# Expert scores of two query tiles in three float32r passes over split q and k, in a kernel with a written-out order

## The chip, the core and the metric

The kernel runs on one core of a Trainium2 chip. Its engines are TensorE (PE; its weight loads are listed as PEld), VectorE (DVE), ScalarE (ACT), GpSimd (POOL) and SyncE (SP), which issues the DMAs. The metric is the time of one execution in microseconds on the device, the median of the runs shown.

## The reference, cut to what matters

An attention layer feeds a layer of four experts that are attention layers themselves. With B = 8 batches, 576 tokens and 8 heads of 64:

```python
scores = scale * np.matmul(q, k.transpose(0, 1, 3, 2))     # local mask in heads 0-3, strided in 4-7
x = softmax(scores) @ v                                    # heads side by side: 8 x 576 x 512
logits = x @ w_gate                                        # the two best of E = 4 experts get weights w
for e in range(E):
    q = x @ wq[e]; k = x @ wk[e]; v = x @ wv[e]            # 576 x 64 each
    scores = scale * (q @ k.transpose(0, 2, 1))            # causal
    a = np.exp(scores - max); a /= a.sum(-1, keepdims=True) + 1e-09
    out += w_e * (a @ v @ wo[e])                           # for tokens that chose e
```

All four experts are computed for all tokens; tokens that did not choose an expert get the weight 0. wq and wk are scaled by 8, so the expert scores are far apart and their precision matters.

## The kernel before, in words

**Stage 1** (`stage1`) computes the first attention for a pair of heads: loads, transposes of q and k, block scores, softmax over the blocks, values. Its result stays in SBUF transposed (512 features on partitions, 576 tokens along the row) as two float32r tiles, `xh` (x rounded to float32r) and `xl` (the remainder), which `split` writes (L746, L748). Weights are split likewise. float32r is a 4-byte type of fewer mantissa bits; a product of two split numbers is computed in three passes, h·h, l·h and h·l (`split3`).

**Stage 2** takes the experts in pairs (ep = 0, 1), the two experts of a pair side by side on partitions 0-63 and 64-127. `project` computes q and k of a pair from x: 12 float32r matmuls (4 feature tiles, three passes) into one PSUM bank for each half of 288 tokens (L934; L946 for the very first), and `pj_out` copies the bank to `qk`, a float32 tile of q and k. `values2` computes v and the gate's logits (L876, L846) and the gate's weights.

`attend` computes the expert scores by tiles of 128 queries and all keys up to the diagonal. Tiles 0 and 1 share one operation (`s2q`, L1001). Tile 2 has 384 keys and tile 3 has 512; each is one operation `s2` (L1013): for each expert a of the pair, one float32 matmul of 64 rows, in the tile shape 64x128, in which the array holds two halves. So there are 8 x 2 x 2 = 32 such operations. The last 64 queries of both pairs share two operations `s2_4` (L1035). Masking and the maximum are one VectorE instruction (L970), the exponential runs on ScalarE (L975), the scaling by the gate's weight on GpSimd (L1070). Then come transposes of the probabilities (L1097), the products with v (L1136), another split, and the output projection (`out_tile`, L1170).

**Order.** Every operation is recorded by `op` with its readers and writers. `schedule` then issues them one by one in the order of the table ORDER, a list of operation numbers; each engine runs its own instructions in that order. SECOND holds the operations that take their second possible engine. FILL says how many filler matmuls (L297) go ahead of a TensorE operation. All PSUM tiles come from one ring of eight banks. The tile shapes that the array is switched between are 128x128, 64x128, 128x64, 64x64, 64x32 and 32x64 (the argument `mode`); a change happens wherever two TensorE operations in a row have different ones.

Of the kernel before, what the change touches and what calls it, by code (L numbers as in the profile page):

```python
# [1246 lines left out]
```

## Time and profile before

| | |
|---|---|
| median of 3 runs | 427.02 us (426.88 to 427.48) |
| profiled execution | 427.57 us |
| its span, first to last instruction | 425.8 us |
| TensorE busy | 415.3 us (98%) |
| VectorE, ScalarE, GpSimd busy | 341.2, 258.0, 209.6 us |
| TensorE clock granted | 1.00 throughout |

The busy times are of one profiled execution. Matmuls overlap in the array and their ends are modelled, so the busy time of TensorE says how long it had something in flight, not how fast it ran. The duration of one matmul record includes its way through the array; what an operation takes of TensorE's time is better read from the chain of waits, where the pieces follow each other without overlap.

### The profile page before, as it was taken

What the parts mean: (1) busy time and instruction counts of PE and PEld (TensorE: products, weight loads), DVE (VectorE), ACT (ScalarE), POOL (GpSimd) and SP (SyncE); (2) the same over time, 40 slices, a digit from 0 to 9 for tenths busy, and PEclk for the clock granted to TensorE, in tenths of its full rate; (3) what the DMA queues carried; (4) which work ended last, traced back from release to release, by engine and by line L of the source; (5) the groups of instructions that cost most, each with busy time, mean ns of one, the idle gap of its engine ahead of it and who ended that gap; (6) DMA issues with size and microseconds to landing.
All of it is one profiled execution on the core that took longest, in us unless ns stands there. A gap on an engine that the chain in (4) does not pass through costs nothing.

```text
span 425.8 us, 18430 instructions
## 1 busy us (share of the span) xinstructions
PE 415.3 (98%) x7464; PEld 354.1 (83%) x7464; DVE 341.2 (80%) x1071; ACT 258.0 (61%) x817; POOL 209.6 (49%) x364
## 2 busy tenths in 40 slices
PE   8889999999999999999999999999999999999996
PEld 5678888997899788997799888988799888988775
DVE  4888999899998998869996789868896877356862
ACT  4677446768665656836776378644477377546741
POOL 5674741757337741584328532576025760281630
PEclk9999999999999999999999999999999999999999
DMA  7846627556556555576244425542551140020033
GB/s 202 213 141 164 123 70 119 115 103 130 86 97 116 104 144 91 107 150 138 42 85 118 93 73 95 85 101 55 126 129 23 51 132 5 4 73 3 25 100 101
DMA packets 156502, 41.86 MB, mean 98 GB/s; under 512 B 146080, under 2 KB 149792, under 8 KB 156416
## 3 DMA queue, kind: packets, MB, share of 16 engines
q1 hardware_dynamic: 156416, 40.67, 43.3%
q8 instruction: 59, 0.97, 1.0%
q14 instruction: 27, 0.22, 0.2%
HBM read 31.20 MB, written 9.44 MB: 95 GB/s over the span
## 4 chain that ended last, share of the span: by engine, by line
PE 81%; DVE 6%; ACT 4%; SPq 4%; POOL 2%; issue 1%; DMA 0%; DVEq 0%; POOLq 0%
PE bank L934 19%; PE bank L1170 11%; PE bank L1136 11%; PE bank L876 8%; PE bank L1097 6%; PE bank L1013 6%; PE bank L764 3%; PE bank L654 3%; PE bank L783 3%; PE bank L1035 2%; PE bank L1001 2%; SPq L570 2%; PE bank L670 2%; SPq L515 2%; PE bank L734 2%; ACT p L975 2%
## 5 line engine op out<-in xcount | busy, mean ns | idle before, releaser
L975 ACT ACTIVATE p<-p,st 128x256 f32<-128x256 f32 (+3 forms) x128 | 71.5, 560 | 16.9 <-DVE st L970 16.8
L1070 POOL TENSOR_SCALAR p<-p,st,wt 128x256 f32<-128x256 f32 (+2 forms) x96 | 63.5, 670 | 31.8 <-DVE st L1061 18.7
L970 DVE CUSTOM_DVE_ANT_0 p<-bank,m_cau 128x384 f32<-128x384 f32 (+2 forms) x96 | 50.1, 549 | 3.4 <-PE bank L1013 2.1
L544 DVE STREAM_TRANSPOSE qkt<-nat 128x576 f32<-128x576 f32 x48 | 47.2, 1003 | 1.8 <-PE bank L654 1.7
L1136 PE MATMUL bank<-th,vs 128*64 128x192 f32 (+4 forms) x512 | 48.2, 337 | 0.1
L1136 PEld LDWEIGHTS bank<-th,vs 128*64 128x64 f32 x512 | 33.9, 137 | 15.8 <-issue 6.5
L337 ACT COPY th<-bank 128x256 f32<-128x256 f32 (+2 forms) x98 | 36.8, 431 | 9.7 <-PE bank L1097 8.5
L697 POOL TENSOR_TENSOR p1l<-p1l,st 128x640 f32<-128x640 f32 (+1 forms) x18 | 20.5, 1143 | 44.8 <-DVE st L695 36.8
L746 ACT CAST xh<-bank 128x128 fp32r<-128x128 f32 (+4 forms) x112 | 28.3, 318 | 23.1 <-PE bank L764 14.8
L876 PE MATMUL bank<-wh_v,xh 128*128 128x260 f32 x128 | 37.1, 289 | 0.3 <-DVE p1s L684 0.3
L748 DVE TENSOR_TENSOR xl<-bank,xh 128x160 fp32r<-128x160 f32 (+4 forms) x112 | 31.9, 320 | 6.6 <-ACT xh L746 6.0
L876 PE MATMUL bank<-wl_v,xh 128*128 128x260 f32 x128 | 36.3, 284 | 0.5 <-DVE wl_v L438 0.5
L1097 PEld LDWEIGHTS bank<-ident,p 64*128 64x128 f32 x800 | 29.8, 138 | 7.6 <-issue 2.7
L934 PE MATMUL bank<-xh,wh_k 128*128 128x288 f32 x120 | 36.0, 300 | 0.1
L876 PE MATMUL bank<-wh_v,xl 128*128 128x260 f32 x128 | 36.0, 282 | 0.0
L934 PE MATMUL bank<-xh,wh_q 128*128 128x288 f32 x120 | 35.6, 297 | 0.0
L934 PE MATMUL bank<-xh,wl_k 128*128 128x288 f32 x120 | 35.3, 295 | 0.0
L934 PE MATMUL bank<-xh,wl_q 128*128 128x288 f32 x120 | 35.3, 294 | 0.0
L934 PE MATMUL bank<-xl,wh_q 128*128 128x288 f32 x120 | 35.3, 294 | 0.0
L934 PE MATMUL bank<-xl,wh_k 128*128 128x288 f32 x120 | 35.3, 294 | 0.0
L337 DVE COPY th<-bank 128x384 f32<-128x384 f32 (+2 forms) x62 | 28.5, 493 | 7.3 <-PE bank L1097 5.4
L1097 PE MATMUL bank<-ident,p 64*128 64x64 f32 x800 | 32.7, 226 | 0.3 <-POOL p L1070 0.2
(184 smaller groups left out, 1171.6 us busy)
## 6 DMA issues: line engine op xcount, KB each, us to landing
nat<-in_q_dram SPq DMA_DIRECT2D x96, 72.0 KB
nat<-in_k_dram SPq DMA_DIRECT2D x96, 72.0 KB
out_dram<-ys SPq DMA_DIRECT2D x23, 256.0 KB
v<-in_v_dram SPq DMA_DIRECT2D x96, 40.0 KB
out_dram<-ys SPq DMA_DIRECT2D x26, 128.0 KB
v<-in_v_dram SPq DMA_DIRECT2D x48, 54.0 KB
v<-in_v_dram SPq DMA_DIRECT2D x32, 48.0 KB
v<-in_v_dram SPq DMA_DIRECT2D x32, 45.0 KB
```

The source lines that it names most:

```text
L337: (nc.scalar.copy if e == "ACT" else nc.vector.tensor_copy)(dst, src)
L544: op("tq", {"DVE": 0.66 if local else 1.11}, k0 - 13, lambda e, x=x: nc.vector.transpose(turned(qkt.t, x), raw(x) if local else raw(x).rea ...
L746: op("xh", {"ACT": act(n_) + 0.04 * (not local)}, key, lambda e, s_=s_, x_=x_: nc.scalar.copy(x_(xh.t), s_(xa.t)), r=[xa], w=[xh[u]])
L748: op("xl", {"DVE": dve(n_)}, key + 0.5, lambda e, s_=s_, x_=x_: nc.vector.tensor_sub(x_(xl.t), s_(xa.t), x_(f(xh.t))), r=[xa, xh[u]], w=[x ...
L876: nc.tensor.matmul(vp.t[:, :NV], xx.t[:, t0:t0 + 128], ww.t[:, kt, :], start=i == 0, stop=i == 11)
L934: nc.tensor.matmul(pj.t[:, :HS], ww.t[:, kt, ep * 128:(ep + 1) * 128], xx.t[:, c], start=i == 0, stop=i == 11)
L970: op("max2", {"DVE": 0.08 + 0.00104 * nk}, k_ + 0.5, lambda e, a=a: nc.vector.tensor_tensor_reduce(out=p.t[:, a, :nk], in0=sp[a].t[:, so:s ...
L975: op("exp2", {"ACT": 0.285 + 0.00084 * nk}, k_ + 1, lambda e, a=a: nc.scalar.activation(p.t[:, a, :nk], p.t[:, a, :nk], AF.Exp, bias=st.t[ ...
L1070: lambda e, p=p, a=a, ci=ci, t=t, nk=nk, s_=s_, ep=ep: nc.gpsimd.tensor_scalar(p.t[:, a, :nk], p.t[:, a, :nk], s_.t[:, 20 + ci + a:21 + ci ...
L1097: nc.tensor.transpose(tp[hf].t[:, 64 * c:64 * c + 64], src, ident[r, r])
L1136: nc.tensor.matmul(acc.t[o, c0:c0 + cn], vw, th[ep, a].t[:, s0:s0 + cn], start=j == 0, stop=j == nj - 1, skip_group_check=True)
L1170: nc.tensor.matmul(yp.t[:, :n_], xx.t[:, c0:c0 + 128], ww.t[:, ep, c], start=i == 0, stop=i == 5)
```

## The change

Tile 2 and tile 3 scores are no longer one float32 matmul per expert but three float32r matmuls over split q and k: (qh, kh), (ql, kh), (qh, kl). For this the halves of q and k are cut at token 256 in place of 288. The first 256 tokens of q and all of k are still copied out as float32 (`qk_lo`; tiles 0, 1 and the last 64 queries use them). The upper 320 tokens of q are written from PSUM as a rounded part (`qk_h`, ScalarE) and a remainder (`qk_l`, VectorE), and their last 64 also as float32 (`q_out`). From the float32 k a rounded part (`k_h`, ScalarE or GpSimd) and a remainder (`k_l`, VectorE or GpSimd) are made for both halves. The split parts lie in a new ring `QKR` of two float32r tiles. The tables SECOND, ORDER and FILL are new; of each a line of before is shown.

```diff
-    HS = S // 2
+    LO = 256
+    CUT = ((0, LO), (LO, S - LO))
...
     batch = [0]
 
     SECOND = {
-        8, 10, 11, 15, 19, 61, 62, 90, 98, 118, 127, 137, 169, 172, 174, 177, 179, 182, 184, 188, 193, 197, 200,
...
     }
     ORDER = [
-        49, 55, 57, 1, 48, 50, 52, 56, 58, 53, 59, 54, 129, 51, 60, 62, 136, 137, 61, 65, 67, 0, 63, 6, 12, 16, 66,
...
     ]
     FILL = {
-        17: 6, 65: 5, 80: 3, 93: 3, 95: 4, 102: 1, 132: 1, 136: 1, 139: 2,
+        7: 1, 17: 7, 80: 4, 132: 3, 134: 3, 139: 1, 216: 2,
     }
 
...
     YS = ring("ys", [128, DM], 3)
-    QK2 = ring("qk2", [128, 2, S], 2)
+    QK2 = ring("qk2", [128, LO + 64 + S], 2)
+    QKR = ring("qkr", [128, 2 * (S - LO) + 2 * S], 2, F32R)
+
+    class QK:
+
+
+        def __init__(self, n):
+            self.lo, self.hl = QK2.new(f"qk_{n}"), QKR.new(f"qkr_{n}")
+
+        def __getitem__(self, i):
+            return (self.hl if i in ((0, 1), "h0", "h1") else self.lo)[i]
+
...
+    def qk_lo(t, j, c, n):
+
+        o = LO + 64 + c if j else c if c < LO else c - S + 64 + LO
+        return t.lo.t[:, o:o + n]
+
+    def qk_hl(t, i, j, c, n):
+
+        o = i * (S - LO) + c - LO if j == 0 else 2 * (S - LO) + i * S + c
+        return t.hl.t[:, o:o + n]
+
+    def passes(t, qc, qn, kc, kn):
+        return [(qk_hl(t, i, 0, qc, qn), qk_hl(t, j, 1, kc, kn)) for i, j in ((0, 0), (1, 0), (0, 1))]
+
     def project(b, ep, qk, nm, key, step):
         j = 0 if nm == "q" else 1
-        for u in range(2):
+        for u, (c0, n_) in enumerate(CUT):
+            c = slice(c0, c0 + n_)
             pj = RB.new(f"pj_{b}_{ep}_{nm}{u}")
 
-            def mm(e, u=u, pj=pj):
-                c = slice(u * HS, (u + 1) * HS)
+            def mm(e, c=c, n_=n_, pj=pj):
                 i = 0
                 for kt in range(KT):
                     for xx, ww in split3(X[b, kt], W[nm]):
-                        nc.tensor.matmul(pj.t[:, :HS], ww.t[:, kt, ep * 128:(ep + 1) * 128], xx.t[:, c],
+                        nc.tensor.matmul(pj.t[:, :n_], ww.t[:, kt, ep * 128:(ep + 1) * 128], xx.t[:, c],
                                          start=i == 0, stop=i == 11)
                         i += 1
 
...
-                op("pj", {"PE": 12 * 0.132}, key + step * u, mm, r=xbufs(b) + wbufs(nm, ep), w=[pj, qk[j, u]], mode=M128)
-            c_ = slice(u * HS, (u + 1) * HS)
-            op("pj_out", either(HS), key + step * u + 0.5, lambda e, c_=c_, pj=pj: copy(
-                e, qk.t[:, j, c_], pj.t[:, :HS]), r=[pj], w=[qk[j, u]])
-
+                op("pj", {"PE": 12 * n_ * 0.00046}, key + step * u, mm, r=xbufs(b) + wbufs(nm, ep), w=[pj, qk[j, u]], mode=M128)
+            k_ = key + step * u + 0.5
+            if u and not j:
+                op("qk_h", {"ACT": act(n_)}, k_, lambda e, pj=pj, n_=n_: nc.scalar.copy(
+                    qk_hl(qk, 0, 0, LO, n_), pj.t[:, :n_]), r=[pj], w=[qk[0, 1]])
+                op("qk_l", {"DVE": dve(n_)}, k_ + 0.1, lambda e, pj=pj, n_=n_: nc.vector.tensor_sub(
+                    qk_hl(qk, 1, 0, LO, n_), pj.t[:, :n_], f(qk_hl(qk, 0, 0, LO, n_))), r=[pj, qk[0, 1]], w=[qk[0, 1]])
+                op("q_out", either(64), k_ + 0.2, lambda e, pj=pj, n_=n_: copy(
+                    e, qk_lo(qk, 0, S - 64, 64), pj.t[:, n_ - 64:n_]), r=[pj], w=[qk[0, 2]])
+                continue
+            op("pj_out", either(n_), k_, lambda e, pj=pj, c0=c0, n_=n_: copy(
+                e, qk_lo(qk, j, c0, n_), pj.t[:, :n_]), r=[pj], w=[qk[j, u]])
+            if j:
+                op("k_h", {"ACT": act(n_), "POOL": 0.1 + 0.001 * n_}, k_ + 0.1, lambda e, c0=c0, n_=n_: (
+                    nc.scalar.copy if e == "ACT" else nc.gpsimd.tensor_copy)(qk_hl(qk, 0, 1, c0, n_), qk_lo(qk, 1, c0, n_)),
+                   r=[qk[1, u]], w=[qk[f"h{u}"]])
+                op("k_l", {"DVE": dve(n_), "POOL": 0.1 + 0.0017 * n_}, k_ + 0.2, lambda e, c0=c0, n_=n_: (
+                    nc.vector if e == "DVE" else nc.gpsimd).tensor_sub(
+                    qk_hl(qk, 1, 1, c0, n_), qk_lo(qk, 1, c0, n_), f(qk_hl(qk, 0, 1, c0, n_))),
+                   r=[qk[1, u], qk[f"h{u}"]], w=[qk[f"h{u}"]])
 
...
                 else:
                     so = 0
-                    us = {(q0 // HS), (q0 + m - 1) // HS}
                     sp = [RB.new(f"s2_{n}_{t}_{a}") for a in range(2)]
 
                     def mm(e, sp=sp, q0=q0, nk=nk, qk=qk):
-                        for a in range(2):
-                            r = slice(64 * a, 64 * a + 64)
-                            nc.tensor.matmul(sp[a].t[:, :nk], qk.t[r, 0, q0:q0 + 128], qk.t[r, 1, :nk], start=True, stop=True)
+                        for i, (qq, kk) in enumerate(passes(qk, q0, 128, 0, nk)):
+                            for a in range(2):
+                                r = slice(64 * a, 64 * a + 64)
+                                nc.tensor.matmul(sp[a].t[:, :nk], qq[r], kk[r], start=i == 0, stop=i == 2)
 
                     op("s2", {"PE": {384: 0.671, 512: 0.886}[nk]}, k_, mm,
-                       r=[qk[0, u] for u in us] + [qk[1, u] for u in range((nk - 1) // HS + 1)],
+                       r=[qk[0, 1], qk["h0"], qk["h1"]],
                        w=[*sp, p[0], p[1]], mode=MR)
...
-                op("s2_4", {"PE": 0.53}, k_ + 0.2 * hh, mml, r=[y for x in qks.values() for y in (x[0, 1], x[1, hh])], w=[*sp, *(p[hh] for p in pl)], mode=MQ)
+                            nc.tensor.matmul(sp[a].t[64 * c:64 * c + 64, :n_], qk_lo(qks[c], 0, S - 64, 64)[h],
+                                             qk_lo(qks[c], 1, c0, n_)[h], start=True, stop=True)
+
+                op("s2_4", {"PE": 0.53}, k_ + 0.2 * hh, mml, r=[y for x in qks.values() for y in (x[0, 2], x[1, hh])], w=[*sp, *(p[hh] for p in pl)], mode=MQ)
...
-        qk = [QK2.new(f"qk_{b}_{ep}") for ep in range(2)]
+        qk = [QK(f"{b}_{ep}") for ep in range(2)]
```

In the numbers of the tables: 22 of the `k_h` go to ScalarE and 10 to GpSimd, 21 of the `k_l` to GpSimd and 11 to VectorE; of the copies out of PSUM, 26 others (net) move from VectorE to ScalarE. FILL sums to 26 before and 21 after. TensorE changes its tile shape 137 times in the order before and 143 times in the order after. The load of the gate's weights is row 18 of SP's order before and row 3 after. In the order after, TensorE has between the last k projection of batch 1's first pair and its tile 2 scores: the value projection of the last tile, a block of local scores and two operations of probability transposes.

On TensorE near the end of the last batch, the scores of tile 3 of the second pair (`qk_153` before, `qkr_155` after). Before, they stand between products with v (L1136) and the output projection (L1170):

```order
L1136 MATMUL bank_67<-th_164,vs_202 64x256
L1136 MATMUL bank_67<-th_165,vs_202 64x128
L1136 MATMUL bank_67<-th_164,vs_202 64x128
L1013 MATMUL bank_65<-qk_153 128x512
L1013 MATMUL bank_71<-qk_153 128x512
L1170 MATMUL bank_66<-wh_o_239,oh_223 128x512
```

After, they stand between the output projection (now L1217) and transposes of probabilities (now L1144):

```order
L1217 MATMUL bank_66<-wl_o_242,oh_224 128x512
L1059 MATMUL bank_65<-qkr_155 128x512
L1059 MATMUL bank_71<-qkr_155 128x512
L1059 MATMUL bank_65<-qkr_155 128x512
L1059 MATMUL bank_71<-qkr_155 128x512
L1059 MATMUL bank_65<-qkr_155 128x512
L1059 MATMUL bank_71<-qkr_155 128x512
L1144 MATMUL bank_67<-ident,p_157 128x64
```

One matmul per expert has become three, the two experts by turns into their two banks, and the operation has moved behind an output projection; the transposes behind it have its own tile shape.

On VectorE in the first batch, around the copies of q and k of the first pair. Before, four copies of 288 columns (L337) stand close together, ahead of the first mask-and-maximum (L970):

```order
L337 COPY qk_152<-bank_67 128x288
L701 TENSOR_REDUCE st_186<-p1l_73 128x10
L337 COPY qk_152<-bank_65 128x288
L337 COPY qk_152<-bank_68 128x288
L337 COPY qk_152<-bank_70 128x288
L970 ISA p_156,st_216<-bank_71,m_cau 128x256
```

After, the remainders of k (L1001) and of q (L989) stand there and one copy (L345):

```order
L1001 TENSOR_TENSOR qkr_154<-qk_152,qkr_154 128x320
L345 COPY qk_152<-bank_66 128x256
L989 TENSOR_TENSOR qkr_154<-bank_65,qkr_154 128x320
L723 TENSOR_REDUCE st_184<-st_184 128x10
L725 RECIPROCAL st_184<-st_184 128x10
L1001 TENSOR_TENSOR qkr_154<-qk_152,qkr_154 128x256
L1016 ISA p_158,st_218<-bank_67,m_cau 128x256
```

Three copies of k and q went to ScalarE, and three subtractions came.

On GpSimd, where the second batch's gate is computed (L906 to L921 before). Before, scalings, a weight's remainder and a softmax step of batch 2 stand there:

```order
L908 TENSOR_TENSOR gt_204<-gt_204,eq_205 128x64
L1070 TENSOR_SCALAR p_158<-p_158,st_218,wt_208 128x384
L697 TENSOR_TENSOR p1l_72<-p1l_72,st_186 128x640
L921 TENSOR_TENSOR wt_209<-wt_209,mx_207 128x4x4
L1070 TENSOR_SCALAR p_161<-p_161,st_219,wt_208 128x512
L438 TENSOR_TENSOR wl_o_240<-ys_150,wh_o_239 128x512
L697 TENSOR_TENSOR p1s_174<-p1s_174,st_188 128x12x54
```

After, two remainders of k of batch 1's first pair (L1001, `qkr_154`) stand each ahead of a softmax step of batch 2 (L716):

```order
L927 TENSOR_TENSOR gt_206<-gt_206,eq_207 128x64
L1001 TENSOR_TENSOR qkr_154<-qk_153,qkr_154 128x256
L716 TENSOR_TENSOR p1s_176<-p1s_176,st_190 128x12x54
L1117 TENSOR_SCALAR p_157<-p_157,st_221,wts_215 128x128
L940 TENSOR_TENSOR wt_211<-wt_211,mx_209 128x4x4
L1001 TENSOR_TENSOR qkr_154<-qk_153,qkr_154 128x320
L716 TENSOR_TENSOR p1s_179<-p1s_179,st_188 128x12x54
```

The scores of batch 1's first pair wait for these subtractions now, and the softmax steps of batch 2 stand behind them.

## Rows read from the trace of the kernel before

**Rows 1.** The page: engines busy, and the clock by slices in tenths

```profile
PE 415.3 (98%) x7464; PEld 354.1 (83%) x7464; DVE 341.2 (80%) x1071; ACT 258.0 (61%) x817; POOL 209.6 (49%) x364
...
PEclk9999999999999999999999999999999999999999
```

**Rows 2.** Stretches: length; busy PE, PEld, DVE, ACT, POOL; clock, DMA share, GB/s

```profile
0.00:60.00 60.00, 54.53 (x1114) 45.29 (x1114) 48.10 (x142) 35.75 (x103) 36.32 (x80) 1.00 0.63 159
60.00:160.00 100.00, 99.42 (x2043) 84.82 (x2043) 93.96 (x278) 63.53 (x205) 53.56 (x84) 1.00 0.57 110
160.00:310.00 150.00, 149.97 (x2805) 130.11 (x2804) 123.74 (x391) 91.73 (x291) 70.85 (x116) 1.00 0.47 96
...
400.00:425.80 25.80, 21.75 (x220) 16.98 (x219) 12.80 (x34) 9.27 (x25) 8.36 (x14) 1.00 0.30 93
```

**Rows 3.** The chain of waits, shares of the span: by engine, by line

```profile
PE 81%; DVE 6%; ACT 4%; SPq 4%; POOL 2%; issue 1%; DMA 0%; DVEq 0%; POOLq 0%
```

```profile
by line: PE bank L934 18.6%; PE bank L1170 11.3%; PE bank L1136 10.7%; PE bank L876 8.5%; PE bank L1097 6.1%; PE bank L1013 5.9%; PE bank L764 3.2%; PE bank L654 3.0%; PE bank L783 2.7%; PE bank L1035 2.2%; PE bank L1001 1.9%; SPq L570 1.9%
```

**Rows 4.** Chain in order of time (start, us, what): scores of tiles 2 and 3

```profile
155.74 0.91 PE bank L1013 x4
...
156.90 1.56 PE bank L1013 x8
...
282.58 0.76 PE bank L1013 x4
```

**Rows 5.** Chain: projections of q and k, v, output

```profile
76.02 1.58 PE bank L934 x12
77.60 1.44 PE bank L876 x12
...
81.52 1.64 PE bank L876 x12
...
184.94 1.40 PE bank L1170 x6
...
405.04 1.59 PE bank L1170 x6
```

**Rows 6.** Groups by line and shape, L1013: count, busy us, mean ns, idle before

```profile
L1013 PE MATMUL bank<-qk 64*128 64x512 f32 x64 | 17.5, 619 | 0.0
L1013 PE MATMUL bank<-qk 64*128 64x384 f32 x64 | 14.3, 516 | 0.0
```

```profile
L1013 PEld LDWEIGHTS bank<-qk 64*128 64x128 f32 x128 | 10.8, 188 | 1.8 <-issue 0.6 <-DVE ol L1149 0.2
```

**Rows 7.** Start: fillers in the chain; issue of the gate's weights

```profile
11.11 1.30 PE bank L297 x6
```

```profile
11.09 0.43 SPq L450 DMA_DIRECT2D w_gate<-in_moe_w_gate_dram  x1
```

**Rows 8.** Groups by line and shape: ScalarE, VectorE, GpSimd

```profile
L337 ACT COPY qk<-bank 128x288 f32<-128x288 f32 x38 | 14.4, 401 | 16.8 <-PE bank L934 15.5 <-DVE mx L903 1.2
L746 ACT CAST xh<-bank 128x324 fp32r<-128x324 f32 x16 | 7.4, 468 | 2.0 <-PE bank L783 1.4 <-DVE st L1041 0.6
L436 ACT CAST wh_q<-th 128x256 fp32r<-128x256 f32 x4 | 1.6, 404 | 0.0
```

```profile
L337 DVE COPY th<-bank 128x384 f32<-128x384 f32 x29 | 15.1, 551 | 3.8 <-PE bank L1097 3.7
L337 DVE COPY qk<-bank 128x288 f32<-128x288 f32 x26 | 11.3, 441 | 6.6 <-PE bank L934 6.6
L748 DVE TENSOR_TENSOR xl<-bank,xh 128x324 fp32r<-128x324 f32 x16 | 7.7, 487 | 0.8 <-ACT xh L746 0.7
```

```profile
L697 POOL TENSOR_TENSOR p1s<-p1s,st 128x648 f32<-128x648 f32 x14 | 17.9, 1280 | 9.2 <-DVE st L695 8.9 <-DVE xl L748 0.3
L438 POOL TENSOR_TENSOR wl_q<-th,wh_q 128x256 fp32r<-128x256 f32 x4 | 3.1, 781 | 0.5 <-ACT wh_q L436 0.5
```

**Rows 9.** Chain: local scores, probability transposes, values of the last tile

```profile
80.62 0.90 PE bank L654 x58
...
86.33 0.90 PE bank L1097 x24
...
180.30 1.44 PE bank L846 x12
```

More of the change, by code (lines that the diff above doesn't have):

```diff
@@ L359, in attention_moe_kernel @@
     m_cau = const.tile([128, S], F32, name="m_cau")
-    m_last = const.tile([128, HS], F32, name="m_last")
+    m_last = const.tile([128, S - LO], F32, name="m_last")
     m_sw = const.tile([128, 128], F32, name="m_sw")
@@ L395, in lasts @@
         for hf in range(2):
-            keep(m_last[64 * hf:64 * hf + 64, HS - 64:], [[-1, 64]], 0, 1)
+            keep(m_last[64 * hf:64 * hf + 64, S - LO - 64:], [[-1, 64]], 0, 1)
         nc.gpsimd.memset(tie, 1.0)
@@ L941, in project, with part @@
                 for kt in START:
-                    def part(e, u=u, pj=pj, kt=kt, left=left):
-                        c = slice(u * HS, (u + 1) * HS)
+                    def part(e, c=c, n_=n_, pj=pj, kt=kt, left=left):
                         left.remove(kt)
                         for i, (xx, ww) in enumerate(split3(X[b, kt], W[nm])):
-                            nc.tensor.matmul(pj.t[:, :HS], ww.t[:, kt, ep * 128:(ep + 1) * 128], xx.t[:, c],
+                            nc.tensor.matmul(pj.t[:, :n_], ww.t[:, kt, ep * 128:(ep + 1) * 128], xx.t[:, c],
                                              start=len(left) == 3 and i == 0, stop=not left and i == 2)
-                    op("pj", {"PE": 3 * 0.132}, key + step * u + 0.1 * kt, part,
+                    op("pj", {"PE": 3 * n_ * 0.00046}, key + step * u + 0.1 * kt, part,
                        r=[X[b, kt][i][x] for i in range(2) for x in range(4)] + wbufs(nm),
@@ L1000, in mmq @@
                                     q_ = c0 + 64 * h
-                                    nc.tensor.matmul(sp[a].t[64 * x:64 * x + 64, c0:c0 + nq], qk.t[r, 0, q_:q_ + 64],
-                                                     qk.t[r, 1, :nq], start=True, stop=True)
+                                    nc.tensor.matmul(sp[a].t[64 * x:64 * x + 64, c0:c0 + nq], qk_lo(qk, 0, q_, 64)[r],
+                                                     qk_lo(qk, 1, 0, nq)[r], start=True, stop=True)
                         op("s2q", {"PE": 0.58}, k_, mmq, r=[qk[0, 0], qk[1, 0]], w=[*sp, *(p2[ep, i][a] for i in range(2) for a in range(2))], mode=MQ)
@@ L1028, in attend, with mml @@
                 sp = [RB.new(f"s2_{b}_l{a}{hh}") for a in range(2)]
-                c0 = hh * HS
-                def mml(e, sp=sp, c0=c0):
+                c0, n_ = CUT[hh]
+                def mml(e, sp=sp, c0=c0, n_=n_):
                     for c in range(2):
@@ L1034, in mml @@
                             h = slice(64 * a, 64 * a + 64)
-                            nc.tensor.matmul(sp[a].t[64 * c:64 * c + 64, :HS], qks[c].t[h, 0, S - 64:], qks[c].t[h, 1, c0:c0 + HS], start=True, stop=True)
-                op("s2_4", {"PE": 0.53}, k_ + 0.2 * hh, mml, r=[y for x in qks.values() for y in (x[0, 1], x[1, hh])], w=[*sp, *(p[hh] for p in pl)], mode=MQ)
+                            nc.tensor.matmul(sp[a].t[64 * c:64 * c + 64, :n_], qk_lo(qks[c], 0, S - 64, 64)[h],
+                                             qk_lo(qks[c], 1, c0, n_)[h], start=True, stop=True)
+                op("s2_4", {"PE": 0.53}, k_ + 0.2 * hh, mml, r=[y for x in qks.values() for y in (x[0, 2], x[1, hh])], w=[*sp, *(p[hh] for p in pl)], mode=MQ)
                 for a, p in enumerate(pl):
                     ci, cs = 2 + a, 4 + a
-                    op("max2_4", {"DVE": 0.1 + 0.00104 * HS}, k_ + 0.5 + 0.2 * hh,
-                       lambda e, sp=sp[a], p=p, c0=c0, hh=hh, ci=ci, cs=cs: nc.vector.tensor_tensor_reduce(
-                           out=p.t[:, c0:c0 + HS], in0=sp.t[:, :HS], in1=m_last if hh else m_cau[:, :HS],
+                    op("max2_4", {"DVE": 0.1 + 0.00104 * n_}, k_ + 0.5 + 0.2 * hh,
+                       lambda e, sp=sp[a], p=p, c0=c0, n_=n_, hh=hh, ci=ci, cs=cs: nc.vector.tensor_tensor_reduce(
+                           out=p.t[:, c0:c0 + n_], in0=sp.t[:, :n_], in1=m_last if hh else m_cau[:, :n_],
                            scale=-SCALE, scalar=sl.t[:, cs:cs + 1] if hh else BIG, op0=ALU.add, op1=ALU.min,
```

287 rows, old and new, of tables (ORDER, SECOND) are left out of this document.

## The prediction

> **What bounds the kernel now.** I read the table of engines first. TensorE is busy for 415.3 of 425.8 us and its granted clock is at the upper level (2.4 GHz) in every slice [rows 1]. A busy matmul engine need not be a full one, so I read the stretches next: between 60 and 310 us TensorE is busy for 249.4 of 250 us, VectorE for 217.7, ScalarE for 155.3, GpSimd for 124.4; TensorE's gaps lie before 60 us (5.5 us) and after 400 us (4.1 us, the last copy and store) [rows 2]. In the first hundred microseconds of that middle VectorE is the second engine, at 94% [rows 2]. Last I read the chain of waits. It runs along TensorE for 81% of the span, and the line of the change, L1013, holds 5.9% of it, which is 25.1 us [rows 3]. What is taken out of TensorE's instruction stream between 60 and 420 us therefore shortens the run almost one for one, as long as the other engines deliver in time.
>
> **The scores, the term that decides.** One score operation of tile 2 (384 keys) with one of tile 3 (512 keys) right behind it takes 1.56 us of the chain; alone they take 0.76 and 0.91 us, with a change of tile shape on one side or none [rows 4]. There are 16 of each, so 16 x 1.56 = 25.0 us, which agrees with the 25.1 us above. Of the 1.56 us, 4 x (384 + 512) columns at one column per clock of 2.4 GHz are 1.493 us; 0.067 us is entry. That uses the columns of one half of the array only: the other half (the second expert of the pair) has no time of its own, so the two halves run beside each other. That the call is split is seen in the 64 records per shape for 32 calls [rows 6].
>
> After the change each half does three float32r matmuls in place of the float32 one, 3 x 896 = 2688 columns. No row of before has float32r in a half array. The nearest are float32r in the full array: 1.58 us for 12 x 288 columns, 1.44 us for 12 x 260, 1.40 us for 6 x 512 [rows 5], that is 0.457, 0.462 and 0.456 ns a column, a tenth above one clock. With 0.457 ns: 2688 x 0.457 = 1.228 us, and 0.067 us entry, 1.295 us. Gain 0.265 us, times 16: **4.2 us**.
> Upper bound: one column per clock as in float32, 1.120 + 0.067 us, gain 0.373 x 16 = 6.0 us. Lower bound: the halves no longer overlap at this rate, 2 x 1.228 + 0.067 = 2.52 us, a loss of 0.96 x 16 = 15.4 us. I take 4.2 us: the rate is that of the same kind of matmul, and the overlap is that of the same tile shape.
>
> The Trainium skill (FP8 and Floating Point Precision, section TensorE Precision Notes) states that true float32 makes four passes through the array. Counted by passes alone, three in place of four, the gain would be a quarter of 25.0 us, 6.2 us; the full-array rows put it at 4.2 us, because they show the float32r column to be dearer.
>
> **Projections, last tile, masks.** The halves of q and k are cut 256/320 in place of 288/288. Each column costs 0.457 ns in either cut, so 576 columns cost the same; the last tile's scores keep their 576 columns too. I count 0, within 0.3 us either way.
>
> **Changes of tile shape.** In the two orders, TensorE goes from one tile shape to another 137 times before and 143 times now. A value projection costs 1.64 us behind another shape and 1.44 us behind its own; an output projection 1.59 against 1.40 us [rows 5]: 0.2 us each. 6 x 0.2 = **1.2 us** more. Bounds 0.5 to 1.5 us, since a boundary inside one shape may cost its 0.067 us as well.
>
> **Start.** The fillers of L297 fall from 26 to 21; six take 1.30 us and stand in the chain [rows 7], 0.217 us each, 1.1 us in all. They stand where TensorE waits for loads or for the first softmax steps, so I count half, **-0.5 us**, with 0 and -1.1 us as bounds. The order now issues the gate's weights in row 3 of SP's order instead of row 18; that issue took 0.43 us on SP's queue [rows 7], and every load behind it, the q of the second head pair first, is up to that much later. The filler covers it (seven now stand before the first local scores); uncovered it is +0.4 us. I count 0.
>
> **Other engines.** ScalarE gains 16 casts of q (nearest row 0.468 us), 22 of k (0.404 us), and of the copies out of PSUM 36 of q and k and some 21 large others where it had 38 (0.401 us): about +24 us, 282 of 424 us. VectorE gains 16 remainders of q and 11 of k (0.487 us each, 13.1 us) and gives up nine copies of q and k (0.441 us), eleven of the rest being of 64 columns only, and the 21 others (0.551 us the dearest): net 0 to +4 us. GpSimd gains 21 remainders of k (0.781 us for 256 columns) and 10 casts: about +22 us, 232 of 424 us [rows 8]. TensorE's 410 us cover all three in total. What counts is the place. A k half now goes through a copy (0.401 us), a cast (0.404) and a remainder (0.781 on GpSimd; 0.98 for 320 columns by the column) before its scores may start: 1.6 to 1.8 us where it was 0.4. The tightest place that I found is batch 1, first pair: between its last k projection and its tile 2 scores TensorE has one last-tile value projection (1.44 us), one local score block (0.90) and two probability transposes (0.90 together) [rows 9], 3.2 us. Cover remains 1.4 us. Queued behind that remainder on GpSimd is a softmax step of batch 2 (1.28 us [rows 8]), for which ScalarE's exponential of that head pair waits; it moves by the remainder's 0.98 us at most. If the cover fails, TensorE stands still, since everything behind a score operation in its queue waits too. I count 0 here; the cost if it fails is a rival.
>
> **Sum.** The profiled execution took 427.57 us (span 425.8 and 1.8 around it). -4.2 + 1.2 - 0.5 = -3.5 us gives 424.1 us; the median of the runs shown is 0.55 us below the profiled one, so **423.5 us**.
>
> **Rivals.**
> *Full rate.* The half array takes a float32r column per clock, as it takes a float32 one. For it: the float32 halves do exactly that [rows 4]. Against it: every float32r row is a tenth dearer [rows 5]. Gain 6.0 in place of 4.2 us: 421.7 us.
> *The preparation comes late or VectorE fills up.* For it: VectorE at 94% between 60 and 160 us [rows 2], and ScalarE, VectorE and GpSimd in a row before each score. Against it: the net on VectorE is small and the cover is 1.4 us or more. If six of the 32 score operations stood for one remainder of 0.78 us, 4.7 us: 428.2 us; if three, 425.8 us.
> *The halves stop overlapping* (the other side). Place: L1013's successors, all 16 pairs of tiles. Price 15.4 us, so 427.0 + 15.4 + 0.7 = 443 us. For it: float32 spends four column times per key, so its rows never show two halves each taking a new key every clock. Against it: local scores and values, in four row groups and more, show several small matmuls in one column time already (a block of local scores, 72 matmuls of 64 columns, takes 0.90 us [rows 9]; one after another at one column per clock they would take 1.92 us). It decides the sign once more than a quarter of the second half's time shows: 3.5 of 15.4 us.
> *Weight loads come into the open.* A load of this shape takes 0.188 us [rows 6], and each half now loads three times per score operation, six times per pair of tiles. Against it: today's four loads per half and pair of tiles leave only 0.067 us for entry [rows 4], so they hide behind matmuls of the same half. If none of the six serial loads hid: 1.228 + 6 x 0.188 = 2.36 us, a loss of 0.80 x 16 = 12.8 us, 440.5 us. The Trainium skill (TensorE: Matmul & The Clock Gate, part 3, The mechanism) says that a load overlaps a running matmul only where the row group differs; by that rule this rival would hold, and the 1.56 us row disagrees with it.
>
> **How the numbers follow.** Forecast as summed 0.70, with its own range 421 to 426 us (gain of the scores 3.5 to 6, shape changes 0.5 to 1.5, start and small stalls 1.5 either way). Full rate 0.11. Late preparation 0.13, half of it above the old time. Halves in turn 0.04, open weight loads 0.02. A difference of 0.2%, 0.85 us, is about what this measurement can tell. Faster by more: 0.66 of the forecast, 0.11, and 0.03 of late preparation, 0.80. Within 0.2%: 0.04 and 0.04, 0.08. Slower: 0.06 of late preparation and 0.06 of the last two, 0.12. The range reaches from 420.5 us (full rate with a better start) to 428.5 us (late preparation).
>
> **What would show it.** In the profile after: L1059 with 96 records of either shape, the two halves starting together, and a chain piece of both tiles of about 1.30 us (1.19: full rate; 2.4 or more: one of the last two rivals); L1059's share of the chain near 20.7 us; TensorE busy for over 99% between 60 and 400 us; no wait of TensorE on the remainders above 0.5 us (else: late preparation); GpSimd near 232 and ScalarE near 282 us. The prediction is wrong if the score pieces aren't shorter, or if they are and TensorE's gaps in the middle grow by more than 2 us.

## The result and the profile after

The changed kernel takes 423.19 us (median of 4 runs, 422.71 to 423.60) against 427.25 us for the kernel before, measured beside it; the ratio is 0.990, 95% interval 0.9878 to 0.9922. That is 4.06 us less; 423.5 us was forecast. The profiled execution took 422.71 us, span 421.0 us; it was the fastest of the four.

The engines over the whole execution (busy us, share of the span, instructions), against [rows 1]:

```profile
PE 410.0 (97%) x7523; PEld 358.3 (85%) x7523; DVE 339.8 (81%) x1073; ACT 277.6 (66%) x877; POOL 231.0 (55%) x398
```

TensorE gives up 5.3 us of busy time, ScalarE takes 19.6 and GpSimd 21.4 us more, VectorE 1.4 less. The stretches of [rows 2] (length; busy PE, PEld, DVE, ACT, POOL; clock, DMA share, GB/s):

```profile
0.00:60.00 60.00, 54.52 (x1205) 45.31 (x1205) 48.69 (x150) 37.48 (x107) 37.36 (x86) 1.00 0.65 164
60.00:160.00 100.00, 99.17 (x2079) 87.12 (x2083) 92.56 (x274) 69.55 (x223) 59.48 (x91) 1.00 0.57 110
160.00:310.00 150.00, 149.74 (x2855) 133.32 (x2846) 129.14 (x409) 100.77 (x328) 81.06 (x129) 1.00 0.48 97
```

TensorE's idle time before 60 us is the same 5.5 us as before, with five fillers fewer; in the middle it grew by 0.25 us per 100 us at most. The start varies between executions: at 30 us, ahead of the first score operation (42.8 us), the profiled executions of e1, e3, e4, e5, e6 and e8 to e12 (runs of the next section, which share the changed kernel's order and fillers) are 0.1 to 1.1 us behind this one, instruction for instruction on TensorE. The scores of tiles 2 and 3 in the chain of waits (start, us, what), against [rows 4]:

```profile
99.28 1.42 PE bank L1059 x12
...
200.73 1.27 PE bank L1059 x12
...
293.91 1.29 PE bank L1059 x12
```

Twelve records, both tiles: 1.27 to 1.29 us where it was 1.56, and 1.42 behind another tile shape. L1059 holds 5.2% of the chain, 21.9 us (31 of the 32 operations lie in it), against 25.1 us (30 of 32). The same line by shape (count, busy us, mean ns, idle before), against [rows 6]:

```profile
L1059 PE MATMUL bank<-qkr 64*128 64x512 f32 x96 | 15.4, 413 | 0.0
L1059 PE MATMUL bank<-qkr 64*128 64x384 f32 x96 | 12.8, 362 | 0.3 <-DVE p1l L703 0.3
```

There are 96 records of either shape, and the 0.3 us of idle time ahead of them is ended by a softmax step, not by a remainder. In the records at 293.7 us the two halves of a pass start 3 to 4 ns apart and a pass follows the last after 0.175 us (384 keys) or 0.232 us (512): 0.456 and 0.453 ns a column. The new instructions on the other engines, against [rows 8]:

```profile
L987 ACT CAST qkr<-bank 128x320 fp32r<-128x320 f32 x16 | 6.8, 424 | 5.5 <-PE bank L966 4.9 <-PE bank L977 0.5
```

```profile
L989 DVE TENSOR_TENSOR qkr<-bank,qkr 128x320 fp32r<-128x320 f32 x16 | 7.6, 478 | 0.0
L1001 DVE TENSOR_TENSOR qkr<-qk,qkr 128x320 fp32r<-128x320 f32 x7 | 5.0, 720 | 1.2 <-ACT qkr L997 0.9 <-POOL qkr L997 0.3
```

```profile
L1001 POOL TENSOR_TENSOR qkr<-qk,qkr 128x256 fp32r<-128x256 f32 x12 | 8.9, 738 | 0.1
```

A remainder of k of 320 columns takes 0.72 us on VectorE on the mean, one of q of the same size 0.48.

### The profile page after: what moved, and what is told of

It reads as the page before. It is cut to its first block, busy times and chain, and to the rows that moved or that the text cites. A ratio compares the mean times of both kernels' runs of the same rounds, so it can differ in the third digit from the quotient of the medians.

```text
span 421.0 us, 18647 instructions
## 1 busy us (share of the span) xinstructions
PE 410.0 (97%) x7523; PEld 358.3 (85%) x7523; DVE 339.8 (81%) x1073; ACT 277.6 (66%) x877; POOL 231.0 (55%) x398
## 4 chain that ended last, share of the span: by engine, by line
PE 84%; DVE 6%; ACT 4%; POOL 3%; issue 2%; DMA 1%; ACTq 0%; POOLq 0%; DVEq 0%
PE bank L966 21%; PE bank L1217 12%; PE bank L1183 10%; PE bank L895 10%; PE bank L1144 6%; PE bank L1059 5%; PE bank L802 3%; PE bank L783 2%; PE bank L1047 2%; PE bank L673 2%; PE bank L1081 2%; PE bank L689 2%; ACT qkt L345 2%; PE bank L753 2%; PE bank L977 1%
## 5 line engine op out<-in xcount | busy, mean ns | idle before, releaser
L1021 ACT ACTIVATE p<-p,st 128x384 f32<-128x384 f32 (+3 forms) x128 | 71.5, 561 | 10.7 <-DVE st L1016 10.6
L1117 POOL TENSOR_SCALAR p<-p,st,wt 128x256 f32<-128x256 f32 (+2 forms) x96 | 64.4, 678 | 15.0 <-DVE st L1108 7.3
L345 ACT COPY th<-bank 128x256 f32<-128x256 f32 (+2 forms) x108 | 40.4, 433 | 7.7 <-PE bank L1144 7.2
L966 PE MATMUL bank<-xh,wh_k 128*128 128x256 f32 (+1 forms) x120 | 36.3, 303 | 0.0
L966 PE MATMUL bank<-xh,wh_q 128*128 128x256 f32 (+1 forms) x120 | 36.1, 301 | 0.1
L767 DVE TENSOR_TENSOR xl<-bank,xh 128x128 fp32r<-128x128 f32 (+4 forms) x112 | 31.8, 322 | 5.3 <-ACT xh L765 4.9
L966 PE MATMUL bank<-xh,wl_k 128*128 128x256 f32 (+1 forms) x120 | 35.5, 296 | 0.0
L966 PE MATMUL bank<-xl,wh_k 128*128 128x256 f32 (+1 forms) x120 | 35.5, 296 | 0.0
L966 PE MATMUL bank<-xh,wl_q 128*128 128x256 f32 (+1 forms) x120 | 35.5, 296 | 0.0
L966 PE MATMUL bank<-xl,wh_q 128*128 128x256 f32 (+1 forms) x120 | 35.5, 296 | 0.0
L1144 PEld LDWEIGHTS bank<-ident,p 64*128 64x128 f32 x800 | 30.2, 139 | 5.7 <-issue 1.3
L716 POOL TENSOR_TENSOR p1l<-p1l,st 128x640 f32<-128x640 f32 (+1 forms) x18 | 20.7, 1153 | 24.9 <-DVE st L714 24.7
L1144 PE MATMUL bank<-ident,p 64*128 64x64 f32 x800 | 33.8, 226 | 0.6 <-DVE p1l L703 0.3
L727 POOL TENSOR_TENSOR p1l<-p1l,st 128x640 f32<-128x640 f32 (+1 forms) x18 | 20.5, 1144 | 18.8 <-DVE st L725 15.4
```

The costliest lines, as they stand in the source:

```text
L345: (nc.scalar.copy if e == "ACT" else nc.vector.tensor_copy)(dst, src)
L767: op("xl", {"DVE": dve(n_)}, key + 0.5, lambda e, s_=s_, x_=x_: nc.vector.tensor_sub(x_(xl.t), s_(xa.t), x_(f(xh.t))), r=[xa, xh[u]], w=[x ...
L966: nc.tensor.matmul(pj.t[:, :n_], ww.t[:, kt, ep * 128:(ep + 1) * 128], xx.t[:, c], start=i == 0, stop=i == 11)
L1021: op("exp2", {"ACT": 0.285 + 0.00084 * nk}, k_ + 1, lambda e, a=a: nc.scalar.activation(p.t[:, a, :nk], p.t[:, a, :nk], AF.Exp, bias=st.t[ ...
L1117: lambda e, p=p, a=a, ci=ci, t=t, nk=nk, s_=s_, ep=ep: nc.gpsimd.tensor_scalar(p.t[:, a, :nk], p.t[:, a, :nk], s_.t[:, 20 + ci + a:21 + ci ...
L1144: nc.tensor.transpose(tp[hf].t[:, 64 * c:64 * c + 64], src, ident[r, r])
```

## The experiments

Each row compares with the kernel before measured beside it (427.45 to 427.65 us; 427.25 for the change); "to after" sets its difference against the 4.06 us of the change, and is good to about 1 us.

| run | median us | ratio to before, 95% | us to before | to after |
|---|---|---|---|---|
| the change | 423.19 | 0.990 (0.9878 to 0.9922) | -4.1 | |
| e1 float32, new order | 429.38 | 1.0039 (1.0026 to 1.0052) | +1.9 | +6.0 |
| e2 passes, old order | 425.97 | 0.9961 (0.9946 to 0.9976) | -1.5 | +2.5 |
| e3 one pass | 422.42 | 0.9873 (0.9857 to 0.989) | -5.1 | -1.0 |
| e4 preparation twice | 444.54 | 1.0393 (1.0359 to 1.0426) | +17.1 | +21.1 |
| e5 no remainders of k | 421.02 | 0.9849 (0.9829 to 0.9869) | -6.4 | -2.4 |
| e6 halves in turn | 422.84 | 0.9895 (0.9873 to 0.9917) | -4.6 | -0.6 |
| e7 no fillers | 426.15 | 0.9974 (0.9953 to 0.9994) | -1.3 | +2.8 |
| e8 k split to key 511 | 421.88 | 0.9869 (0.9848 to 0.9891) | -5.6 | -1.5 |
| e9 q and k split to 511 | 421.93 | 0.9872 (0.9852 to 0.9891) | -5.7 | -1.7 |
| e10 and k casts on ScalarE | 428.95 | 1.0032 (1.0019 to 1.0045) | +1.3 | +5.4 |
| e11 small matmul, same shape | 426.12 | 0.9962 (0.9949 to 0.9975) | -1.5 | +2.5 |
| e12 small matmul, half shape | 433.76 | 1.014 (1.0125 to 1.0154) | +6.1 | +10.2 |

### The passes and the order, each alone (e1, e2)

```diff
 # e1, in the changed kernel
-for i, (qq, kk) in enumerate(passes(qk, q0, 128, 0, nk)):
-    for a in range(2):
-        ...
-        nc.tensor.matmul(sp[a].t[:, :nk], qq[r], kk[r], start=i == 0, stop=i == 2)
+for a in range(2):
+    ...
+    nc.tensor.matmul(sp[a].t[:, :nk], f(qk_hl(qk, 0, 0, q0, 128))[r], f(qk_hl(qk, 0, 1, 0, nk))[r], start=True, stop=True)
 # e2, in the kernel before
-QK2 = ring("qk2", [128, 2, S], 2)
+QK2 = ring("qk2", [128, 2, S], 2, F32R)
-    nc.tensor.matmul(sp[a].t[:, :nk], qk.t[r, 0, q0:q0 + 128], qk.t[r, 1, :nk], start=True, stop=True)
+    # three times, start=i == 0, stop=i == 2; the other readers take f(qk.t)
```

> The changed kernel with one float32 matmul per half again for tiles 2 and 3, on the rounded parts of q and k (the remainders' terms are left out); casts, remainders, order, fillers as in the changed kernel. Theory 'the passes pay': the piece of both tiles goes from 1.29 back to about 1.56 us, 16 times 0.27 us, so 423.2 + 4.3 = 427.5 us, level with the kernel before. Rival 'the new order and start pay': no more than 0.5 us above the changed kernel, 423.7 us.

> The kernel before with its order, cut and fillers, its copies of q and k rounded to float32r, and three float32r matmuls per half for tiles 2 and 3, all over the same rounded q and k (so the remainders' terms are left out and nothing is added on ScalarE, VectorE or GpSimd). Theory 'the passes pay': 16 times 0.27 us less, 427.3 - 4.3 = 423.0 us. Rival 'the new order and start pay': 427 us. If it lies below 423.0 us, the change loses the rest in its order or preparation.

Measured: e1 6.0 us above the change, e2 1.5 us below the kernel before; e1 goes beyond 'the passes pay' (4.3 us), e2 lies between its two theories. The pieces of the chain are what was expected in both, 1.56 us in e1 and 1.33 (with parts of a neighbour between) in e2:

```profile
204.24 1.56 PE bank L1058 x8
```

```profile
206.15 1.33 PE bank L1014 x12
```

In e1 all of it reaches the end. But for the scores it runs the changed kernel's TensorE instructions in the same order, so each can be set against its counterpart: e1's profiled execution is 1.1 us behind at 45 us, which is nearly all start (0.9 us at 40 us, before any score), and 6.2 us at the end, so 5.1 us belong to what comes after. The scores take 3.8 us more over the records (27.0 for 23.1), and waits of other operations come on top: between 60 and 400 us TensorE stood for 1.7 us before values of the first attention (L802, L783), where the changed kernel didn't stand:

```profile
PE bank L802 <- issue: 1.1, 2, 0.7
PE bank L783 <- issue: 0.6, 1, 0.6
```

In e2 little of it reaches the end, and none before 240 us. Here are the same output projections (count, ns least/median/most, first and last start) of the kernel before and of e2:

```profile
L1170 PE MATMUL bank<-wh_o,oh x2: 392/395/398, 152.8 to 153.5; 128*128 128x512 f32 x2
```

```profile
L1171 PE MATMUL bank<-wh_o,oh x2: 393/394/394, 152.8 to 153.5; 128*128 128x512 f32 x2
```

At 152.8 us both stand at the same place, after nine shorter score operations; at 246.9 us still. The gain comes between 250 and 400 us. In the first part VectorE was 94% busy in the kernel before [rows 2]; the chain's share of VectorE rose from 6% [rows 3] to 10% in e2; that VectorE is what takes the gain back up to 247 us fits this, but no run shows it by itself. So the two halves of the change bring -1.5 us (passes in the old order) and +1.9 us (new order and preparation with float32), and together -4.1 us: they are worth little apart.

### TensorE's stream cut further (e3)

```diff
-for i, (qq, kk) in enumerate(passes(qk, q0, 128, 0, nk)):
+for qq, kk in passes(qk, q0, 128, 0, nk)[:1]:
+    ...   # start=True, stop=True
```

> The changed kernel with only the first of the three passes (rounded q by rounded k) for tiles 2 and 3; the remainders are still prepared. Two passes of a pair of tiles are 2 x (0.175 + 0.232) = 0.81 us less, 16 times. Theory 'TensorE's stream sets the time one for one': 423.2 - 13.0 = 410.2 us. Rival 'another engine is close behind' (VectorE was 93% busy from 60 to 160 us): half of it or less, 416.5 us or more.

Measured: 1.0 us below the change; the rival holds, more strongly than it was put. Summed over the records, from the start of each score operation to that of the next operation, the scores fall from 23.1 to 13.9 us; 3.3 us come back ahead of transposes of the probabilities, 4.4 in the first attention's local scores and values, the rest in smaller pieces. The chain of e3 shows how, at the place where the changed kernel runs scores without a break (293.91 above):

```profile
292.95 1.59 PE bank L1183 x20
...
295.12 0.28 DVE ol L1196
295.40 0.13 DVE xl L767
295.53 0.93 DVE th L345 x2
...
296.50 0.40 PE bank L1144 x6
296.90 0.29 PE bank L1059 x2
```

The chain leaves TensorE and goes through VectorE's queue: remainders, then the copy of transposed probabilities that frees what the next transposes wait for. By engine the chain is

```profile
PE 75%; DVE 12%; ACT 6%; POOL 3%; issue 3%; DMA 1%; POOLq 0%; ACTq 0%
```

with VectorE at 12% where the changed kernel has 6%. TensorE still shows 98% busy between 60 and 400 us: a busy share near 100% doesn't say that its stream sets the time.

### The preparation (e4, e5, e8, e9, e10)

```diff
 # e4: qk_l, k_h and k_l issue their instruction twice; e5: k_l issues none, and the third pass takes kh
 # e8: ahead of k_h and k_l
+n_ = 256
 # e9: e8, and for qk_h and qk_l
+w_ = 256      # in place of n_
 # e10: e9, and
-    nc.scalar.copy if e == "ACT" else nc.gpsimd.tensor_copy)(qk_hl(qk, 0, 1, c0, n_), ...)
+    nc.scalar.copy)(qk_hl(qk, 0, 1, c0, n_), ...)
```

> The changed kernel with every cast of k, every remainder of k and every remainder of q issued twice (GpSimd, VectorE and ScalarE: some 21, 13 and 9 us more work, all of it ahead of the scores of tiles 2 and 3). Theory 'the preparation is hidden': within 0.2% of the changed kernel, 422.4 to 424.1 us. Rival 'it sits close to the path': 426 us or more, with waits of TensorE on the remainders in L1059's rows.

> The changed kernel without the 32 remainders of k: nothing is issued for them, and the third pass reads the rounded k a second time, so TensorE's work stays the same. GpSimd loses about 17 us and VectorE 4 us of work. Theory 'the preparation as it stands is covered': within 0.2% of the changed kernel, 422.4 to 424.0 us. Rival 'the doubled preparation cost 21 us because the single one costs some already': 421 us or less.

> The changed kernel with the casts and remainders of the second half of k cut from 320 to 256 columns (keys 512 to 575 are not read by tiles 2 and 3). Some 1.5 us less on GpSimd and 1 us on ScalarE and VectorE each. Theory 'the preparation is covered': no change, 422.7 to 423.7 us. Rival 'the cover is short in places': up to 1 us faster, 422.2 us.

> The run before this one's cut of k (casts and remainders up to key 511), and the same for q: cast and remainder of 256 in place of 320 queries, since the last 64 have their own float32 copy and tiles 2 and 3 don't read them. 16 x 0.067 = 1.1 us less on VectorE, 0.8 us less on ScalarE, both ahead of the scores. Theory 'the preparation costs TensorE something although little of it shows as idle time' (no remainders of k: 2.2 us less; k cut: 1.3 us less): 0.3 to 0.8 us below the k cut alone, 421.1 to 421.6 us. Rival 'only GpSimd's queue matters': no change to the k cut, 421.9 us.

> Both cuts, and the ten casts of k that GpSimd does moved to ScalarE (some 4 us from GpSimd to ScalarE, at the same places of the order). Theory 'GpSimd's queue holds up the scaling of the probabilities, for which the transposes wait': 0.2 to 0.8 us below the run with both cuts. Rival 'ScalarE's queue is as tight': no change or up to 1 us above it.

Measured: twice costs 21.1 us, none of k gives 2.4 us, k cut to 256 columns (casts and remainders) 1.5 us, the cut of q nothing more (0.15 us between medians of e8 and e9). So 'covered' failed in e4, e5 and e8, and in e9 the rival holds. In e4 TensorE waits for GpSimd, for remainders (L1001) and for scalings queued behind them (L1117), and for VectorE, for remainders of the first attention's result (L767):

```profile
PE bank L1144 <- POOL p L1117: 5.0, 3, 3.1
PE bank L1217 <- DVE xl L767: 2.7, 2, 2.4
PE bank L1059 <- POOL qkr L1001: 2.5, 2, 2.3
```

In the changed kernel no such wait shows, but its chain runs through the preparation in the last batch:

```profile
377.04 0.18 DVE st L1108
377.21 0.44 DVE qk L345 x2
377.65 0.40 DVE qkr L989
378.05 1.12 DVE qkr L1001
379.17 0.41 DVE qkr L989
...
379.63 0.84 PE bank L1144 x19
```

In e5 the chain stays on TensorE there:

```profile
375.68 1.43 PE bank L966 x12
377.10 1.41 PE bank L1142 x40
378.51 1.28 PE bank L1057 x12
```

Five VectorE instructions, 2.37 us, stand between the last softmax step and the transposes; without the remainder of 1.12 us they deliver before TensorE is there.

Set instruction against instruction on TensorE, e5's profiled execution gains 2.9 us on the changed kernel's from 45 us to the end, and only 0.35 us of it here. 0.8 us come at 96 us (the scores of batch 1's first pair), 0.8 us between 142 and 146 us, 0.5 us at 308 and 0.35 us at 345 us. At 96 us it isn't the remainder itself that is late. On GpSimd a remainder stands ahead of a softmax step (L716) and moves it; VectorE's first gate step (L920) then runs beside that step. Changed kernel, GpSimd and VectorE, then e5's VectorE (start, us, instruction, idle before):

```profile
93.77 0.88 POOL L1001 TENSOR_TENSOR qkr<-qk,qkr 128x320 fp32r<-128x320 f32 x1 [0.80 <-ACT qkr L997]
94.59 1.28 POOL L716 TENSOR_TENSOR p1s<-p1s,st 128x648 f32<-128x648 f32 x1
```

```profile
94.77 1.14 DVE L920 TENSOR_TENSOR gt<-lg 128x16 f32<-128x16 f32 x1 [0.22 <-ACT lg L345]
```

```profile
95.64 0.18 DVE L920 TENSOR_TENSOR gt<-lg 128x16 f32<-128x16 f32 x1 [0.22 <-ACT lg L345]
```

The gate step takes 1.14 us in place of 0.18, and the mask step behind it (L703), for which TensorE waits, comes that much later. Between 142 and 146 us it is a remainder on VectorE itself that takes 1.43 us beside GpSimd (see the last section).

e10 moves ten casts at unchanged places and loses 7.0 us against e9, where the theory gave a gain and the rival a loss of up to 1 us: both failed. GpSimd's queue (start, us, instruction, idle before):

```profile
379.21 0.96 POOL L1003 TENSOR_TENSOR qkr<-qk,qkr 128x256 fp32r<-128x256 f32 x1 [4.53 <-ACT qkr L1000]
380.16 1.34 POOL L1119 TENSOR_SCALAR p<-p,st,wt 128x256 f32<-128x256 f32 x2
```

The cast that GpSimd did itself now stands in ScalarE's queue behind a copy that waits 4.6 us for TensorE; the remainder waits 4.53 us for the cast; two scalings stand behind the remainder; and TensorE waits 3.6 us for these. Then the clock falls. The stretches (behind the comma TensorE's busy time; the last but two is the granted clock) and the scores behind them:

```profile
380.00:384.00 4.00, 0.46 (x14) 0.46 (x16) 0.48 (x3) 0.56 (x2) 4.00 (x8) 1.00 0.28 64
384.00:386.00 2.00, 2.00 (x40) 1.81 (x36) 1.79 (x4) 1.53 (x4) 2.00 (x4) 0.66 0.00 0
386.00:388.00 2.00, 2.00 (x12) 1.22 (x10) 1.13 (x3) 0.63 (x2) 1.92 (x5) 0.50 0.00 0
```

```profile
385.19 2.35 PE bank L1061 x12
```

After 4 us with 0.46 us of work the clock was granted at 0.50, its lower level of 1.2 GHz, and the pair of score tiles took 2.35 us in place of 1.28. Wait and clock together put e10's profiled execution 5.2 us further behind e9's between 376 and 384 us; another 1.4 us had come near 100 us, where TensorE waited 0.9 us for a cast of k on ScalarE.

### The two halves of the array (e6)

```diff
-for i, (qq, kk) in enumerate(passes(qk, q0, 128, 0, nk)):
-    for a in range(2):
-        ...
+for a in range(2):
+    ...
+    for i, (qq, kk) in enumerate(passes(qk, q0, 128, 0, nk)):
```

> The changed kernel with the six matmuls of a score operation in another order: all three passes of the first half, then all three of the second, in place of alternating halves. Theory 'TensorE takes its matmuls in the order of its queue, and the overlap comes from alternating': a half's second pass waits for its first, and the other half behind it waits too, so 5 steps in place of 3: 2 x (0.175 + 0.232) = 0.81 us more per pair of tiles, 16 times, 13 us, 436 us; more if the other ops wait too. Rival 'each half runs its own queue': 423.2 us.

Measured: no change (0.6 us, within what can be told). The rival holds. A score operation of 512 keys, first in e6, then in the changed kernel:

```profile
L1059 PE MATMUL bank<-qkr x6: 388/398/501, 394.3 to 394.9; 64*128 64x512 f32 x6
```

```profile
L1059 PE MATMUL bank<-qkr x6: 388/398/501, 394.3 to 394.9; 64*128 64x512 f32 x6
```

Six matmuls in three steps in both, with the starts in pairs, 3 ns apart in the changed kernel and 10 ns in e6 (the most frequent distances over the whole runs too). The records name neither the half nor the place in the queue. Six full passes fit into three steps only if the halves overlap, and the wider distance fits a partner that stands three places behind in place of one. So the halves overlap although, by the kernel's text, all of the first half's passes stand ahead.

### Fillers (e7)

```diff
-        7: 1, 17: 7, 80: 4, 132: 3, 134: 3, 139: 1, 216: 2,
```

> The changed kernel without its 21 filler matmuls (21 x 0.217 = 4.6 us of TensorE). Theory 'they stand where TensorE waits for loads or softmax steps': within 0.4% of the changed kernel and the granted clock unchanged, 421.7 to 423.6 us. Rival 'they stand on the path': 418.6 us. Rival 'they hold the clock up': a granted clock below 1.00 in the first 60 us and 424 us or more.

Measured: 2.8 us above the change; the third theory holds. Of e7, from 5 to 15 and from 25 to 30 us:

```profile
5.00:10.00 5.00, 3.08 (x50) 2.27 (x51) 2.61 (x10) 4.38 (x11) 1.71 (x8) 0.81 0.77 193
10.00:15.00 5.00, 4.67 (x140) 3.84 (x128) 3.94 (x10) 3.17 (x9) 2.21 (x6) 0.51 0.65 199
...
25.00:30.00 5.00, 4.91 (x127) 4.25 (x111) 4.17 (x13) 3.06 (x10) 2.41 (x7) 0.66 0.61 172
```

The granted clock is 0.81, 0.51 and 0.66 there; the changed kernel has 1.00 in all of them. Against the changed kernel's execution e7's is 1.4 us behind at 45 us and 2.5 at 160 us; runs with the fillers were up to 1.6 us behind at 45 us too, so the profile doesn't split the 2.8 us of the medians between the clock and the start's own variation.

### The price of a change of tile shape (e11, e12)

```diff
 # e11, ahead of each output projection
+nc.tensor.matmul(yp.t[:, :64], src[0][0].t[:, c0:c0 + 128], W["o"][0].t[:, 0, :64], start=True, stop=True)
 # e12
+nc.tensor.matmul(yp.t[:, :64], src[0][0].t[:64, c0:c0 + 128], W["o"][0].t[:64, 0, :64], start=True, stop=True)
```

> The changed kernel with one matmul of 64 columns in the full array (128 rows) ahead of each of the 37 output projections, into the bank that the projection then writes anew. It is the control for the next run. 64 columns x 0.457 ns are 0.03 us: 37 x 0.03 = 1.1 us with nothing else, up to 37 x 0.1 = 3.7 us with an entry each: 424.3 to 426.9 us.

> The same with the small matmul on 64 rows (64x128), so 58 more changes of tile shape than in the control (24 projections stood behind a full-array matmul and get two more, 10 behind another shape and get one more, 3 behind 64x128 and get none). Theory 'a change costs 0.2 us': 11.6 us above the control. Rival 'a change costs no more than another entry', 0.07 us: 4 us above it.

Measured: the control 2.5 us above the change (0.07 us each), e12 7.6 us above the control: 0.13 us for each of the 58 changes, between the two theories. Most of them are between the full array and 64x128. In the chain of e11 and of e12 (small matmul, projection):

```profile
304.82 0.03 PE bank L1215
304.85 1.48 PE bank L1218 x6
```

```profile
309.49 0.22 PE bank L1215
309.71 1.58 PE bank L1218 x6
```

0.19 us go into the half shape and 0.10 back, 0.15 on the mean of the two.

## Why the prediction was right, and where it wasn't

**The scores, 4.2 us.** Right in kind and size. The column costs the same tenth above one clock in the half array as in the full one, and the halves start together: a pair of tiles takes 1.27 to 1.29 us (1.295 forecast). Over the records (from an operation's start to that of the next) the 32 operations fall from 27.7 to 23.1 us, 4.6 us. The chain holds 21.9 us instead of 20.7: 17 of its 31 operations stand alone, at 0.58 us or more for 384 keys and 0.75 or more for 512, which is 1.33 us or more for two, and some pairs have another tile shape ahead (1.42 us). The 25.0 us of the prediction met the chain's 25.1 us partly by luck: most operations stand alone before too, at 0.70 and 0.91 us or more, and the chain leaves two of the 32 out. The rivals full rate, halves in turn and open weight loads are out; e6 shows that the overlap doesn't even need the alternating order.

**"Shortens the run almost one for one, as long as the other engines deliver in time".** This step failed as a rule. In the new order it held from float32 to three passes (e1: 3.8 us of scores, 5.1 us of time from 45 us on). It did not hold elsewhere: e2 took 3.7 us out of the score operations (27.7 to 24.0, over the records) and won 1.5, e3 took 9.2 us more out and won 1.0. The chain's 81% on TensorE [rows 3] and its 99% of busy time [rows 2] were read as slack elsewhere; the runs fit an order in which each engine's result arrives just before it is used.

**Changes of tile shape, +1.2 us.** Too dear: six by 0.13 us are 0.8 us, inside the bounds, if the other shapes cost the same. The 0.2 us were read from projections behind one shape or another; between the full and the half shape a change took 0.19 us in and 0.10 back.

**Start, -0.5 us.** Before 60 us TensorE is idle for the same 5.5 us with five fillers fewer, which is the far bound, 1.1 us. That rests on one profiled execution, and other executions of the same start differ by as much. What the prediction had not seen is that fillers hold the clock (e7); the five could go without the clock falling.

**Other engines, 0.** The totals came out on ScalarE (277.6 for 282) and GpSimd (231.0 for 232). VectorE's -1.4 us lies below the range of 0 to +4, which didn't follow from its own prices: 13.1 - 9 x 0.441 - 21 x 0.551 us is -2.4. The term was mis-sized all the same: the remainders of k alone cost 2.4 us (e5), and casts and remainders of 64 columns that nothing reads 1.5 us (e8). So the rival of late preparation was in part true, inside a run that gained. The place was found, batch 1's first pair, but not the mechanism: 0.8 us are lost there, not because the cover of 1.4 us fails, but because the remainder moves a softmax step on GpSimd beside VectorE's gate. And a remainder of k on VectorE was priced at 0.487 us; the eleven took 0.41 to 1.43 us, and the two slowest, 1.43 and 1.20 us, stand where e5 gains 0.8 and 0.35 us. That no wait of TensorE above 0.5 us on the remainders shows, as forecast, does not mean that they are free.

**The sum.** -3.5 us forecast, -4.1 measured. With the sizes found, -4.6 + 0.8 - 1.1 + 2.4 = -2.5 us; the missing 1.6 us are put down to the new order by difference alone. That the passes and the order are worth more together than apart is shown by e1 and e2 as a pair (+1.9 and -1.5 apart, -4.1 together); which of the moves brings it was not tried. The records show where the 4.8 us of the span went, from each start to the next: scores -4.6, fillers -1.1, transposes of the probabilities in both stages +1.5, all other operations -0.7 together, with the value projections at -1.2 and the projections of q and k at +0.8. So the forecast came near in part by luck: preparation at nothing and the order at nothing are two errors that cancelled.

**A better version.** e8 beats both kernels: 421.88 us (421.58 to 422.22), 1.3% below the kernel before; its interval overlaps that of the change by 0.0013, but its slowest run lies below the fastest of the change, and from 45 us on its profiled execution gains 1.3 us on that of the change. It computes the same, since tiles 2 and 3 don't read the keys left out.

## What to carry to other kernels

In a kernel with a written-out order, a shorter operation on the busiest engine is worth its time only as far as the other engines' results can come earlier too; price it together with the order, and test it alone in the old order before believing either number. Work "hidden" on another engine stands in that engine's queue ahead of something: follow the queue to who waits behind it, look at what it moves beside another engine's instructions, and cut the columns that nobody reads. Where two runs share an order, set instruction against instruction: that shows where time is gained, which the chain of one run doesn't. Fillers and waits are to be read with the granted clock beside them: in e10 a wait of 3.6 us was paid a second time afterwards.
